# Three down products per gated chunk by a second level of Strassen's seven products

## The chip, the cores and the metric

The kernel runs on one core of a Trainium2 chip. The metric is device time in microseconds (us) for one execution, the median of several. The profile is of one execution of the same program; its durations are read against its own span.

## The reference

Four layers run over x, 2048 tokens of width 1024: attention, gated, attention, gated. Each adds to x what it computes from the LayerNorm of x.

```python
def _A_ref(x, wqkv, wo):            # linear attention, 32 heads of 32
    q, k, v = ...                   # (x @ wqkv), split into heads
    phi = lambda t: jnp.where(t > 0, t + 1, jnp.exp(t)) + 1e-6
    pq, pk = phi(q), phi(k)
    kv = jnp.einsum("bhsd,bhse->bhde", pk, v)
    z = jnp.einsum("bhsd->bhd", pk)
    num = jnp.einsum("bhqd,bhde->bhqe", pq, kv)
    den = jnp.einsum("bhqd,bhd->bhq", pq, z)[..., None] + 1e-6
    return (num / den) @ wo         # heads joined again

def _B_ref(x, W_gate, W_up, W_down):     # F = 3584
    gate = x @ W_gate
    gate = gate * (gate > 0)
    return (gate * (x @ W_up)) @ W_down

x = x + _A_ref(_layernorm(x), ...)
x = x + _B_ref(_layernorm(x), ...)
x = x + _A_ref(_layernorm(x), ...)
x = x + _B_ref(_layernorm(x), ...)
```

## The kernel before, in words

`run` (L1274) takes the layers in order: `layer_A(0)`, `layer_B(1)`, `layer_A(2)`, `layer_B(3)`. The residual x stays in SBUF as sixteen tiles of 128 tokens (L145), f32, 1024 wide.

A gated layer (`layer_B`, L1212) works on two chunks c = 0, 1 of 1024 tokens each. A chunk has two stages. In the gate/up stage a loop over u = 0 to 13 calls `glu` (L1063): each u makes 2 x 128 columns of F for both weights, with Strassen's seven products on blocks of 4 contraction tiles, and leaves four 128x512 blocks of h = relu(gate) * up in a tile hT[u // 2], f16, kept transposed (F on partitions, tokens on columns). So h has four blocks: a = first 512 tokens with the first half of F (in the order of the weight's tiles), b = first tokens, second half, g and d = the same for the second 512 tokens.

Then `down` (L1146) multiplies h by W_down, again with one level of Strassen: the chunk's 1024 x 3584 by 3584 x 1024 is cut into 2 x 2 blocks each way, and seven block products are summed. A product, `product` (L1168), is 4 banks (one per 128 tokens) x 14 contraction tiles = 56 matmuls of 128x128 by 512 columns, in two halves of 7 tiles, one ring entry per half. Their names: "11", "21", "22" use blocks of W_down as they are, T1, T2, T3, T4 use sums of weight blocks, made once in layer 1's chunk 0 (`sums_d`, L1002) and stored in DRAM as `td`. The order is 11, 21, T1, T2, T3, 22, T4. Product 11 goes to banks X, which ScalarE copies to banks Y (`seed`); 21 adds to X; T2, T3 and T4 add to Y; T1 and 22 use four banks V. After a product that completes a result, or a part of one, `add_down` (L1261) adds each bank onto x with one VectorE add of 512 columns, or in the last layer forms a bf16 tile and sends it out. VectorE makes the sums of h's blocks at the start of down (L1156 to L1159): e1 = g + d, e2 = e1 - a, and a - g in place of g, and after product 21 has read it b - e2 in place of b (L1193).

What sets the order: TensorE's instructions keep program order. The framework orders the other engines' queues by when things become ready, except where `issue_after` ties an instruction behind another one or a manual schedule is named. A list of later tasks (`_Later`, L71) runs host-side closures a number of ticks later; a tick is one small group of matmuls, 8 per down product. All weights come through one ring (`_Ring`, L24), depth 5: at the start of an entry's use, the load of the entry four ahead is issued on SP's queue, as soon as a slot is free. Ring entries, h, sums, transposed LayerNorm outputs and others share one pool of 16 slots of 8 KB per partition (`big`). SP's queue also takes the DMA transposes of LayerNorm's output (L397) and copies of x rows to DRAM and back (`send_away`, `bring_back`). PSUM has eight banks: four in `ps`, two in `ps3`, two in `kvp`.

In layer 1, chunk 1, the gate/up stage also makes weight sums for layer 2's projections (`load_w`, `sums_w`, L1015 and L1024): eight VectorE sums of 2048 elements, each placed behind the last put of h.

Of the kernel before, what the change touches and what calls it, by code (L numbers as in the profile page):

```python
# [8 lines left out]
ALU = mybir.AluOpType  # L9
ACT = mybir.ActivationFunctionType  # L10
F32 = mybir.dt.float32
BF16 = mybir.dt.bfloat16
F16 = mybir.dt.float16
PSUM = bass.MemoryType.PSUM
P = 128
NW = 512
HD = 32
QT = 4
# [5 lines left out]
class _Ring:  # L24


    def __init__(self, nc, slot, depth):
        self.nc, self.slot, self.depth = nc, slot, depth
        self.plan, self.tiles, self.loaded = [], {}, 0
# [63 lines left out]
class _Net:  # L93
    def __init__(self, tc, ctx, x_d, wqkv_d, wo_d, wg_d, wu_d, wd_d, out_d):
        nc = tc.nc
        self.tc, self.nc = tc, nc
        _, S, D = x_d.shape
        self.S, self.D = S, D
        self.ST, self.KT = S // P, D // P
        self.G = D // P  # L100
        self.F = wg_d.shape[1]
        self.FT = self.F // P
        self.NQ = self.ST // QT
        self.x_v = x_d.rearrange("b (st p) d -> p (b st) d", p=P)
        self.o_v = out_d.rearrange("b (st p) d -> p (b st) d", p=P)
        self.wqkv_v = wqkv_d.rearrange("(kt p) n -> p kt n", p=P)
        self.wo_v = wo_d.rearrange("(kt p) n -> p kt n", p=P)
        self.wgu_v = {"g": wg_d.rearrange("(kt p) f -> p kt f", p=P),
                      "u": wu_d.rearrange("(kt p) f -> p kt f", p=P)}
        self.wd_v = wd_d.rearrange("(u h p) n -> p h u n", p=P, h=2)  # L110
        self.U = self.F // (2 * P)

        pool = lambda name, bufs, **kw: ctx.enter_context(tc.tile_pool(name=name, bufs=bufs, **kw))
        self.const = pool("const", 1)
        self.xres = pool("xres", 1)
        self.big = pool("big", 16)
        self.ep = pool("ep", 7)
        self.small = pool("small", 4)
        self.ps = pool("ps", 4, space=PSUM)
        self.ps3 = pool("ps3", 2, space=PSUM)  # L120
        self.kvp = pool("kvp", 1, space=PSUM)


        self.spill = pool("spill", 1, space=bass.MemoryType.DRAM)
        self.NS = self.ST // 2
        self.ring = _Ring(nc, self.slot, 5)
        self.tgu = {(w, u): self.spill.tile([P, 4, NW], F16, name=f"t{w}{u}")
                    for w in "gu" for u in range(self.U)}
        self.td = self.spill.tile([P, self.U, 4, NW], F16, name="td")
        self.tw = {n: self.spill.tile([P, 8, NW], F16, name=f"t{n}") for n in ("q0", "q1", "k0", "k1")}  # L130
        self.later = _Later()
        self.phi_lag = 0

        from concourse.masks import make_identity
        self.ident = self.const.tile([P, P], BF16, name="ident")
        make_identity(nc, self.ident[:, :])
        self.ones = self.const.tile([P, P], BF16, name="ones")
        nc.vector.memset(self.ones, 1.0)
        self.mean = 2.0 ** -11
        assert self.S == 2 ** 11  # L140
        self.eps6 = self.const.tile([P, 1], F32, name="eps6")
        nc.vector.memset(self.eps6, 1e-6)
        self.eps5 = self.const.tile([P, 1], F32, name="eps5")
        nc.vector.memset(self.eps5, 1e-5)
        self.x = [self.xres.tile([P, D], F32, name=f"x{t}") for t in range(self.ST)]  # L145

        self.xb = [x[:, D // 2:D].bitcast(BF16) for x in self.x]
        self.xnT, self.xn, self.pk, self.slabs, self.xs, self.acc = {}, {}, {}, {}, {}, {}
        self.away = [self.spill.tile([P, D], F32, name=f"away{t}") for t in range(self.ST)]
# [803 lines left out]
    def plan_B(self, l):  # L953
        for c in range(2):
            for u in range(self.U):
                for w in "gu":
                    self.ring.add((l, c, w, u), lambda t, w=w, u=u, first=(l == 1 and c == 0):
                                  self.load_gu(t, w, u, first))
            for p in ("11", "21", "T1", "T2", "T3", "22", "T4"):
                for h in range(2):  # L960
                    us = slice(h * self.U // 2, (h + 1) * self.U // 2)
                    if p[0] == "T":
                        src = self.td[:, us, self.T_AT[p], :]
                    else:
                        n = int(p[1]) - 1
                        src = self.wd_v[:, int(p[0]) - 1, us, n * NW:(n + 1) * NW]
                    self.ring.add((l, c, p, h), lambda t, src=src: self.nc.sync.dma_start(
                        out=t[:, 0:self.U // 2, :].bitcast(src.dtype), in_=src))

    T_AT = {"T1": 0, "T3": 1, "T4": 2, "T2": 3}  # L970

    def raw_gu(self, t):
        return t[:, 0:4, :].rearrange("p a (b f) -> p (a b) f", f=2 * P)
# [89 lines left out]
    def glu(self, l, c, u, hT):  # L1063
# [74 lines left out]
        for w in "gu":  # L1138
# [4 lines left out]
            else:  # L1143
                put(2, Y[w])

    def down(self, l, c, hT, final):  # L1146


        nc, later, ring, v = self.nc, self.later, self.ring, self.nc.vector
        N = NW  # L1150
        pairs = [(p, [x[:, b::4, :] for b in range(4)]) for p, x in enumerate(hT)]
        e1, e2 = ([self.slot(f"e{i}_{l}_{c}_{k}", dtype=F16) for k in range(2)] for i in (1, 2))
        part = lambda e, p: e[p // 4][:, (p % 4) * 2:(p % 4) * 2 + 2, :]
# [6 lines left out]
        raw = lambda b: lambda k: hT[k // 2][:, (k % 2) * 4 + b, :]  # L1160
        own = lambda e: lambda k: e[k // 8][:, k % 8, :]
        X = [self.ps.tile([P, N], F32, tag="a", name=f"dx{j}") for j in range(QT)]
        Y = [self.ps3.tile([P, N], F32, tag="b", name=f"dy{j}") for j in range(2)]
# [48 lines left out]
    def layer_B(self, l, final):  # L1212
        ring = self.ring

        def behind(it, fn):
            with self.tc.issue_after(it.ins):
                fn()

        for c in range(2):
            hT = []  # L1220
            first = l == 1 and c == 0
            wd = {}
            for u in range(self.U):
                if u % 2 == 0:
                    hT.append(self.slot(f"h{l}_{c}_{u // 2}", dtype=F16))
                ring.load_to(ring.index((l, c, "g", u)) + 5)
                if first:
                    if u + 1 < self.U:
                        self.later.at(4 if u else 9, lambda u=u: behind(self.last_put if u else self.last_z, lambda: [
                            self.make_gu(ring.get((l, c, w, u + 1)), w, u + 1) for w in "gu"]))  # L1230
                    if u in (3, 7):
                        d = self.U - 4 + u // 4 * 2
                        wd[d] = self.load_d(d)
                    if 3 < u < 12:
                        self.later.at(4, lambda d=self.U - 4 + (u - 4) // 4 * 2, n=(u - 4) % 4: behind(
                            self.last_put, lambda: self.sums_d(wd[d], d, (n,))))
                if not final and c == 1:
                    if u in (0, 3):
                        self.load_w("qk"[u // 3])
                    if u in (1, 2, 4, 5):  # L1240
                        for n in range(2):
                            self.later.at(4 + 5 * n, lambda w="qk"[u // 4], n=2 * (u % 3 - 1) + n: behind(
                                self.last_put, lambda: self.sums_w(w, n)))
                if c == 0 and u == 1:
                    for n, turn in enumerate(self.turns):
                        self.later.at(1 + n, turn)
                if c == 0 and u in (1, 2):
                    self.later.at(6, lambda u=u: behind(self.last_put, self.pairs[u - 1]))
                self.glu(l, c, u, hT)
                if c == 0 and u == 2:  # L1250
                    self.pairs[2]()
                if c == 0 and u == (self.U - 1 if first else 0):
                    after = self.last_put.ins
            if c == 0:
                self.ln_chunk(l, 1, 20, 3, 3, after)
            elif not final:
                self.ln_later(l + 1, 0, 28, 3, 4)
                self.ln_later(l + 1, 1, 40, 3, 4)
            self.down(l, c, hT, final)
# [71 lines left out]
```

## Time and profile before

| | |
|---|---|
| median of 3 runs | 1461.36 us (1461.35 to 1461.69) |
| span of the profiled execution | 1459.6 us; the median lies 1.8 us above it |
| down, layer 1, chunk 1 | 650.84 to 735.44 us |
| down, layer 3, chunks 0 and 1 | 1117.79 to 1202.40 and 1371.61 to 1456.23 us |
| TensorE's clock granted | 1.00 |
| DMA | 268.09 MB, 184 GB/s on the mean |

Starts are from the span's start. In the group rows, "mean ns of one" is from an instruction's start to its end; neighbours on an engine overlap, so the pace of a stream is read from the chain or the timeline, as the difference of two starts. "Idle before" with an arrow names what released the engine.

### The profile page before, as it was taken

Reading aid. Unit: us, or ns where it says so; the run is one execution under the profiler, and the core shown is the slowest. Engines: PE = TensorE matmul, PEld = TensorE weight load, DVE = VectorE, ACT = ScalarE, POOL = GpSimd, SP = SyncE. Lnnn points to the kernel's source line nnn. Section 1 sums busy time; section 2 is a strip of 40 time slices with the busy share of each in tenths; the row PEclk is TensorE's granted clock in tenths of the full one; section 3 lists DMA queues with packets and bytes.
Section 4 is the critical chain, followed back from the end, with each engine's and each line's share of the span. In section 5 each row is a group of like instructions: output and inputs, shape, how many; then the busy total and the mean of one; then the engine's idle time right before and its main releaser. Section 6 shows DMA issues by size and latency. Waiting matters only on the chain.

```text
span 1459.6 us, 18713 instructions
## 1 busy us (share of the span) xinstructions
PE 1453.7 (100%) x6926; PEld 659.9 (45%) x6926; DVE 869.9 (60%) x1547; ACT 579.6 (40%) x1041; POOL 287.2 (20%) x190
## 2 busy tenths in 40 slices
PE   9999999999999999999999999999999999999999
PEld 4444444444444444444444444444444444444444
DVE  7978698666684554456388876776436433333632
ACT  7872564333340333340068626524333203333200
POOL 1454851011100011110031586401110001111000
PEclk9999999999999999999999999999999999999999
DMA  9840897564559996445943129975444787444461
GB/s 285 232 162 11 182 218 202 184 217 161 205 171 253 354 291 223 149 132 189 278 141 88 58 37 290 261 228 167 146 147 148 196 261 243 146 149 149 147 200 44
DMA packets 323915, 268.09 MB, mean 184 GB/s; under 512 B 106096, under 2 KB 295920, under 8 KB 321904
## 3 DMA queue, kind: packets, MB, share of 16 engines
q1 hardware_dynamic: 312800, 245.60, 57.2%
q10 hardware_dynamic: 11024, 21.30, 3.9%
q8 instruction: 54, 0.88, 0.3%
q14 instruction: 37, 0.30, 0.1%
HBM read 203.42 MB, written 38.80 MB: 166 GB/s over the span
## 4 chain that ended last, share of the span: by engine, by line
PE 96%; DVE 3%; ACT 1%; issue 0%; DMA 0%; DVEq 0%; ACTq 0%
PE ps L477 11%; PE dy L1177 10%; PE yu L1078 10%; PE yg L1078 10%; PE dv L1177 7%; PE dx L1177 7%; PE xg L1078 6%; PE xu L1078 6%; PE ps L755 4%; PE zg L1078 3%; PE zu L1078 3%; PE vu L1078 3%; PE vg L1078 3%; PE my L559 3%; PE mx L559 2%; PE mv L559 2%
## 5 line engine op out<-in xcount | busy, mean ns | idle before, releaser
L1078 PEld LDWEIGHTS <-w 128*128 128x128 f16 (+1 forms) x3136 | 306.6, 98 | 372.0 <-issue 2.5
L1131 POOL TENSOR_TENSOR h<-m5u,m5g 128x512 f16<-128x512 f32 x56 | 71.9, 1285 | 810.7 <-DVE m5u L1127 754.6
L477 PE MATMUL ps<-w,xnT 128*128 128x512 bf16 x768 | 169.8, 379 | 0.1
L1177 PEld LDWEIGHTS <-h 128*128 128x128 f16 x1120 | 109.6, 98 | 132.2
L1114 DVE TENSOR_TENSOR zg<-yg,m5g 128x512 f32<-128x512 f32 x56 | 39.1, 699 | 188.9 <-PE yg L1078 185.6
L1078 PE MATMUL yg<-s,w 128*128 128x512 f16 x448 | 115.0, 379 | 0.1
L1078 PE MATMUL yu<-s,w 128*128 128x512 f16 x448 | 115.0, 379 | 0.0
L1078 PE MATMUL xg<-xnT,w 128*128 128x512 f16 x448 | 115.0, 379 | 0.0
L1078 PE MATMUL xu<-xnT,w 128*128 128x512 f16 x448 | 115.0, 379 | 0.0
L477 PEld LDWEIGHTS <-xnT 128*128 128x128 bf16 x768 | 74.3, 98 | 89.8 <-issue 1.4
L1086 ACT ACTIVATE m5g<-m5g 128x512 f32<-128x512 f32 x56 | 35.2, 628 | 174.8 <-DVE m5g L1127 174.8
L1177 PE MATMUL dy<-w,h 128*128 128x512 f16 x448 | 98.0, 379 | 0.0
L1177 PE MATMUL dx<-w,h 128*128 128x512 bf16 x448 | 97.3, 379 | 0.0
L420 ACT ACTIVATE e<-e,eps 128x512 f32<-128x512 f32 x128 | 90.9, 720 | 3.3
L707 POOL TENSOR_TENSOR kvc<-pq,kvc 128x1024 f32<-128x1024 bf16 x32 | 78.6, 2455 | 53.1 <-DVE den L712 32.8
L755 PE MATMUL ps<-T,pqT 128*128 128x512 bf16 x384 | 83.6, 379 | 0.0
L1095 ACT ACTIVATE m5g<-vg 128x512 f32<-128x512 f32 x56 | 33.4, 597 | 110.9 <-PE vg L1078 85.2
L498 POOL TENSOR_TENSOR kvc<-kvc,slab 128x512 f32<-128x512 f32 x46 | 57.2, 1249 | 75.9 <-DVE slab L423 72.7
L1089 DVE TENSOR_TENSOR h<-yu,r 128x512 f16<-128x512 f32 x56 | 38.7, 691 | 56.0 <-PE yu L1078 56.0
L1127 DVE TENSOR_TENSOR m5u<-yu,m5u 128x512 f32<-128x512 f32 x56 | 38.7, 691 | 49.4 <-PE yu L1078 49.4
L1177 PEld LDWEIGHTS <-e 128*128 128x128 f16 x448 | 43.8, 98 | 52.9
L1086 ACT ACTIVATE r<-yg 128x512 f32<-128x512 f32 x56 | 33.4, 597 | 86.0 <-PE yg L1078 86.0
(198 smaller groups left out, 2129.9 us busy)
## 6 DMA issues: line engine op xcount, KB each, us to landing
w<-in_B_W_gate_dram SPq DMA_DIRECT2D x56, 512.0 KB, 5.9
w<-in_B_W_up_dram SPq DMA_DIRECT2D x56, 512.0 KB, 5.4
w<-td SPq DMA_DIRECT2D x32, 896.0 KB, 4.7
w<-in_B_W_down_dram SPq DMA_DIRECT2D x24, 896.0 KB, 5.2
w<-tg SPq DMA_DIRECT2D x42, 512.0 KB, 6.9
w<-tu SPq DMA_DIRECT2D x42, 512.0 KB, 6.7
w<-in_A_wqkv_dram SPq DMA_DIRECT2D x8, 1024.0 KB, 7.3
away<-x SPq DMA_DIRECT2D x16, 512.0 KB, 5.3
```

The lines of the kernel that those rows point to most:

```text
L420: nc.scalar.activation(out=e, in_=e, func=ACT.Exp, scale=-1.0, bias=self.eps6[:, 0:1])
L477: nc.tensor.matmul(by_row(ps), lhsT=self.xnT[l, l_q][:, kt, j * P:(j + 1) * P], rhs=w[:, kt, :].rearrange("p (b i d) -> p i b d", i=R, d=H ...
L498: nc.gpsimd.tensor_tensor(out=ksum[:, cols], in0=ksum[:, cols], in1=pk, op=ALU.add)
L559: nc.tensor.matmul(banks[j], lhsT=A(i)[:, j * P:(j + 1) * P], rhs=B(i), start=start and i == 0, stop=i == NS - 1, skip_group_check=True)
L707: nc.gpsimd.tensor_tensor(out=prod, in0=pq_of[sc, j], in1=zrow, op=ALU.mult)
L755: nc.tensor.matmul(ps, lhsT=pqT[sc][:, g, j * P:(j + 1) * P], rhs=T[g // 4][:, g % 4, n2 * NW:(n2 + 1) * NW], start=(g == 0), stop=(g == G ...
L1078: nc.tensor.matmul(ps, lhsT=W[w][m][:, k, :], rhs=A[m][:, k, :], start=start and k == 0, stop=k == 3, skip_group_check=True)
L1086: self.last_relu = nc.scalar.activation(out=out, in_=ps, func=ACT.Relu)
L1089: self.last_put = nc.vector.tensor_tensor(out=h[:, b, :], in0=ps, in1=R.pop(b), op=ALU.mult)
L1114: self.last_z = nc.vector.tensor_tensor(out=Z[w], in0=Y[w], in1=V[w], op=ALU.add)
L1131: nc.gpsimd.tensor_tensor(out=h[:, 3, :], in0=V["u"], in1=V["g"], op=ALU.mult)
L1177: nc.tensor.matmul(banks[j], lhsT=A(k)[:, j * P:(j + 1) * P], rhs=w[:, i, :], start=start and k == 0, stop=k == self.U - 1, skip_group_che ...
```

## The change

In three of the four gated chunks (all but layer 1's chunk 0) `down` calls a new `down_deep`. There T1, 22 and T4 are each computed by a second level of seven products. The block of h (512 tokens x 14 tiles) and the block of the weight (14 tiles x 512 columns) are cut in 2 x 2 again: an inner product is 2 banks' halves x 7 tiles = 14 matmuls of 128x128 by 256 columns, both 128-token halves in one bank. VectorE makes four inner sums of the h block, each in four pieces, into the space of h's block a, which is no longer needed after product 11. The order of the outer products becomes 11, 21, T1, T2, 22, T3, T4.

The inner weight sums (four per product) are made in layer 1's chunk 1, during gate/up: at u = 1, 4, 7 a weight block is loaded into two slots (`load_dd`), at u = 2, 3, 5, 6, 8, 9 two sums each are made (`sums_dd`) and stored in new DRAM tensors `dd`. A deep product takes four ring entries in place of two, seven DMAs in place of two. x becomes one SBUF tile with sixteen views, so that a put can add 2 x 256 columns of two token tiles at once.

```diff
+        self.dd = {p: self.spill.tile([P, 4, self.U // 2, NW // 2], F16, name=f"dd{p}") for p in self.DEEP}
...
-        self.x = [self.xres.tile([P, D], F32, name=f"x{t}") for t in range(self.ST)]
+        self.xall = self.xres.tile([P, self.ST, D], F32, name="x")
+        self.x = [self.xall[:, t, :] for t in range(self.ST)]
...
-            for p in ("11", "21", "T1", "T2", "T3", "22", "T4"):
+            for p in self.order_d(l, c):
+                if self.is_deep(l, c, p):
+                    for e in range(4):
+                        self.ring.add((l, c, p, e), lambda t, p=p, e=e: self.load_deep(t, p, e))
+                    continue
...
+    DEEP = ("T1", "22", "T4")
...
+    def sums_dd(self, p, n):
+        t = self.deep_t
...
+        self.nc.vector.tensor_tensor(out=out, in0=a, in1=b, op=ALU.subtract)
+        if n == 1:
+            self.later.at(2, lambda: [self.nc.sync.dma_start(out=self.dd[p][:, m, :, :], in_=f16(b))
+                                      for m, b in ((0, b11), (2, b12))])
...
+    def down_deep(self, l, c, hT, final):
...
+        def inner(A):
+            (a11, a21), (a12, a22) = ([cut(A[k], j) for j in range(2)] for k in range(2))
+            return (a11, a12, a21, a22), list(sums(((S1, a21, a22, ALU.add), (S2, S1, a11, ALU.subtract),
+                                                    (S3, a11, a21, ALU.subtract),
+                                                    (S4, a12, S2, ALU.subtract))))
...
+            def mm(m, A, bank, start=False):
+                for j in range(2):
+                    for i in range(NK):
+                        nc.tensor.matmul(bank[:, j * H:(j + 1) * H],
+                                         lhsT=A[i // 2][:, i % 2, j * P:(j + 1) * P], rhs=B[m](i),
+                                         start=start and i == 0 and j == 0, stop=i == NK - 1,
+                                         skip_group_check=True)
+
+            x, y, z = (self.ps.tile([P, N], F32, tag="a", name=f"d{n}{p}") for n in "xyz")
+            m5 = self.temp(name="dm5")
+            copy = lambda out, src: nc.scalar.activation(out=out, in_=src, func=ACT.Copy)
+            entry(0)
+            mm(1, a11, x, True)
+            copy(y, x)
+            later.tick()
+            mm(5, S1, z, True)
+            copy(m5, z)
+            later.tick()
+            entry(1)
+            mm(6, S2, y)
+            v.tensor_tensor(out=z, in0=y, in1=m5, op=ALU.add)
+            later.tick()
+            mm(2, a12, x)
+            put(0, 0, x, True)
+            put(1, 1, m5, False)
+            later.tick()
+            entry(2)
+            mm(7, S3, y)
+            put(1, 1, y, True)
+            later.tick()
+            mm(3, S4, z)
+            put(0, 1, z, True)
+            later.tick()
+            entry(3)
+            mm(4, a22, y)
+            put(1, 0, y, True)
+            later.tick()
...
+        product("11", raw(0), X, True, seed)
+        product("21", raw(1), X, False, to(first, 0, X, True))
+        for p, (_, b, _, _) in pairs:
+            v.tensor_tensor(out=b, in0=b, in1=part(e2, p), op=ALU.subtract)
+        parts, jobs = inner(of_e(e1))
+        for job in jobs:
+            job()
+        deep("T1", parts, put_both)
+        parts, jobs = inner(of_h(1))
+        spread(jobs, 1, 2)
+        product("T2", own(e2), Y, False, to(first, 1, Y, False))
+        deep("22", parts, put_into(first, 1))
+        parts, jobs = inner(of_h(3))
+        spread(jobs, 1, 2)
...
+        product("T3", raw(2), Y, False, third_done)
+        deep("T4", parts, put_into(second, 0))
...
+                if not final and c == 1:
+                    if u in (1, 4, 7):
+                        self.later.at(1, lambda p=self.DEEP[u // 3]: self.load_dd(p))
+                    if u in (2, 3, 5, 6, 8, 9):
+                        for n in range(2):
+                            self.later.at(2 + 5 * n, lambda p=self.DEEP[(u - 2) // 3], n=2 * ((u - 2) % 3) + n: behind(
+                                self.last_put, lambda: self.sums_dd(p, n)))
```

In `deep`, T1 puts each result onto both halves of the chunk (`put_both`, two adds), 22 and T4 onto one; `third_done` adds T3's banks onto two places. All of these are adds of 512 elements per partition onto x by VectorE, or the output tile in the last layer.

## The prediction

> **What bounds the kernel now.** I read the page's busy shares first, then the chain that ended last, then the groups with shapes kept apart, then the timeline and the stretches around the gated chunks' down products.
>
> ```profile
> PE 1453.7 (100%) x6926; PEld 659.9 (45%) x6926; DVE 869.9 (60%) x1547; ACT 579.6 (40%) x1041; POOL 287.2 (20%) x190
> PE 96%; DVE 3%; ACT 1%; issue 0%; DMA 0%; DVEq 0%; ACTq 0%
> 675.01 12.09 PE dv L1177 x56
> 147.92 0.89 PE kv L514 x16
> L514 PE MATMUL kv<-mt,w 128*128 128x128 bf16 x128 | 8.5, 219 | 0.0
> L514 PEld LDWEIGHTS <-w 128*128 128x128 bf16 x128 | 7.8, 98 | 1.9
> ```
>
> TensorE is the bound: busy all of the 1459.6 us, 96% of the chain. So matmul time taken away is span taken away, unless TensorE then waits. The durations (379 ns, 219 ns) are latencies that overlap; the pace is in the chain. One of the seven down products, 56 matmuls of 512 columns, takes 12.09 us, 215.8 ns each. The sixteen 128-column matmuls of L514 take 0.89 us, 55.6 ns each, each with its own weight load.
>
> ```profile
> 735.76 0.68 DVE L1265 TENSOR_TENSOR x<-x,dy 128x512 f32<-128x512 f32 x1
> 736.36 0.42 DVE L1053 TENSOR_TENSOR s<-s,xnT 128x512 f16<-128x512 f16 x1
> 736.70 0.69 DVE L160 BATCH_NORM_STATS2 stats<-x 128x6 f32<-128x512 f32 x1
> ...
> 499.84 1.22 DVE L1031 TENSOR_TENSOR wq<-wq,wq 128x2048 f16<-128x2048 bf16 x1
> 500.97 0.69 DVE L1114 TENSOR_TENSOR zu<-yu,m5u 128x512 f32<-128x512 f32 x1
> ...
> 501.72 1.02 PE L1078 MATMUL yu<-s,w 128*128 128x512 f16 x4
> ```
>
> This gives VectorE's pace: an f32 add of 512 holds the queue 0.60 us (done after 0.69), an f16 sum of 512 holds it 0.34. And it shows what a late bank costs: the 1.22 us sum pushed the zu add to 500.97, done 501.66, and TensorE went on at 501.72, 0.06 us later; its step before (zg at 500.69) should have ended at 501.55, so 0.16 us were lost.
>
> ```profile
> 675.00:687.00 12.00, 12.00 (x58) 5.45 (x56) 5.49 (x9) 0.00 (x0) 0.00 (x0) 1.00 0.47 154
> 518.00:530.00 12.00, 12.00 (x58) 5.46 (x56) 4.68 (x8) 4.67 (x8) 1.27 (x1) 1.00 1.09 349
> 578.00:590.00 12.00, 12.00 (x57) 5.42 (x56) 4.86 (x7) 4.58 (x9) 1.24 (x1) 1.00 0.55 175
> ```
>
> Columns: stretch, length, busy PE, PEld, DVE, ACT, POOL, clock, DMA share, GB/s. During product T1 of layer 1 VectorE works 5.5 of 12 us. In the gate/up part of the same chunk DMA is full (1.09 at 349 GB/s) early and half full (0.55, 175 GB/s) later.
>
> **Removed: matmul time.** Nine products (T1, 22 and T4 in three chunks) go from 56 matmuls of 512 columns to 7 x 2 x 7 = 98 of 256. No row of the trace has 256 columns. Between L514's 55.6 ns and L1177's 215.8 ns the straight line gives 109.0 ns, 98 x 109.0 = 10.68 us, 1.40 us saved per product, **12.6 us in all**. The rule that speaks against this: the Trainium skill, "TensorE: Matmul & The Clock Gate", section "Back-to-back issue gap", says that a stream of weight load and matmul pairs sustains only about 81 ns at 128 columns, not 56. By that rule 256 columns would cost about 109 + 25 = 134 ns (an estimate from that page), a product 13.1 us, and the change would lose 9 us before anything else. The row has such pairs at 55.6 ns, so I take 109; but it has only 16 in a row, so the rule stays as a rival.
>
> **Added on VectorE in down.** Per chunk 24 adds onto x become 33 plus 3 into z and 3 more for T3's second target, 39 (15 more, 9.0 us), and 48 inner sums come (per product twelve of 0.34 and four of 256 elements, about 0.20 by the same slope: 4.8 us, 14.4 in three). VectorE had 46 us in the 84 us of down in layer 1; with 23 more it still fits, but not everywhere. The built program's VectorE order places T1's inner sums before product 21's adds (they need only product 11 to be over): 21 sums of 1024 at 0.60 and these 4.8 us end about 18 us into the 24 us of 11 and 21. Hidden; without that cover TensorE would wait up to 5 us there, three times.
>
> What is not hidden are the banks used again inside a deep product, with steps of 1.53 us in the order 1, 5, 6, 2, 7, 3, 4. Step 7 writes the bank that the z add after step 6 reads; step 4 writes the one that the put after step 7 reads. The spare step between is 1.53 us, and ahead of both reads other work stands in VectorE's queue. Walk T1 of layer 3, t from its first matmul, 0.2 us from a step's end to VectorE's start (1137.47 against 1137.27 in the timeline): leftovers of 21 (four h updates at 0.60 and one add) last to 2.3; the S1 sums for product 22, which wait for step 5 (3.25), to 4.45; two puts of m5 to 5.65; z done at 6.34. Step 7 is due at 6.10, goes at 6.40: 0.3 lost. Then three S2 sums to 7.25, two puts of x to 8.45, two sums to 9.0, two puts of y, done 10.27; step 4, due 9.46, goes at 10.33: 0.87 lost. Together 1.17. T1 of layer 1 has two statistics in place of sums: 0.89. Product 22 puts once, not twice: z done 6.41 (0.37 lost), y done 9.56 (0.09): 0.46. T4 has no sums beside it: 0. Sum: 0.89 + 2 x 1.17 + 3 x 0.46 = **4.6 us back**. Queued behind those waits are only puts and sums that T2 and T3, 12 us each on other banks, absorb.
>
> Product 22 moves ahead of T3: its h blocks were updated during T1, and T3's banks then have a whole product in which T2's adds read them; down has 53 ticks instead of 56, so LayerNorm's steps and their transposes on SP shift by a tick or two, with layer 2's first use of them after the end of down. Cost 0.
>
> ScalarE gets two copies of 0.58 us per product. Each has the 1.53 us of the next step as cover, and LayerNorm's 1.24 us activations stand behind them in its order; cost 0. POOL does nothing in down.
>
> **Added in layer 1, chunk 1, gate/up.** Twelve sums of 1792 elements for the stored inner weights; from L1031's 1216 ns for 2048, about 1.08 us, 0.99 in the queue. In the place where L1031 lost 0.16 us a 0.99 us sum loses 0.03, so by themselves 0.4 at most. But each waits for its load, and VectorE's puts wait behind it. The loads and stores are 3 x (1.8 + 1.8) MB, some 11 MB, on SP's queue among the ring's loads, in a stretch whose first half is already at 350 GB/s. Following SP's order at 350 GB/s, every "up" block still lands 2 to 7 us before its turn; the second raw pair (22) lands near 545.4 and 547.9, while the sums stand ahead of a z add due at 547.1. I take 1.0 us. Ends: 0 (all in time; I see no gain) and 8 us (each of three pairs some 2.7 us late).
>
> **Added DMA in down.** A deep product brings 3.1 MB, not 1.8, in seven DMAs in place of two: 4 MB more in 80 us per chunk. A ring load is issued four entries ahead; deep entries last 3 us, so the lead falls from 24 us to 10.7 at least. Rows of 512 bytes are no novelty: the 512 KB gate blocks land in 5.9 us. What gets close is the hand-over to the next stage: layer 2's k0 is now issued when T4 starts, 10.7 us ahead (35 us before the change), with a landing of 8.7 us in that stretch, and transposes of about 2 us each stand between k0 and k1 on SP. I take 0.6 us for both hand-overs; ends 0 and 5. At the very end the last add is split in two as before: 0. Making x one tile leaves the waits of the other stages as they were in the built order: 0.
>
> Sum against the profiled execution: 1459.6 - 12.6 + 4.6 + 1.0 + 0.6 = 1453.2 us of span. The median lies 1.8 us above that span, so **1455.0 us**. About 0.2% (2.9 us) is what a measurement of this kernel can tell from no change.
>
> **Rivals.** (A) As summed, 1453 to 1458: 0.50. (B) The banks come free in time, since the order in the queue bends with real landings: stalls under 1.5 us and no late DMA, 1448.8 to 1452: 0.18. For it: T4's pattern loses nothing; against: the walk has 5 to 6 us of queue between steps 5 and 7. (C) DMA: the stored sums and the hand-over take most of the bounds above, 5 to 10 us, as the share of 1.0 and more suggests: 1458.4 to 1464: 0.18. Against: the ring's 12 to 24 us of lead. (D) The slower one, a single mechanism: the 256-column stream is paced by its weight loads. A product breaks even at 12.09/98 = 123 ns, the whole change at (9 x 12.09 - 6.2)/882 = 116 ns. At the skill's 134 ns: 9 x (13.13 - 12.09) = +9.4, with 6.2 of stalls 1477: 0.14 with all that goes with it (several late DMAs beyond their bounds, 1465 and more). That fewer columns are not streamed is excluded: the built program has 756 more TensorE rows, that is 9 x 42 pairs.
>
> Chances: faster by over 0.2% (below 1458.4) 0.68, within 0.2% 0.18, slower 0.14. The range takes in A, B and C: 1449 to 1464.5.
>
> **What would show it.** In the changed profile: 256-column matmuls of T1, 22 and T4, with T4 at 10.7 us in the chain (right) or 12 and more (D); TensorE waiting on VectorE's z add and puts in T1 and 22, about 0.5 to 1.2 us each, and none in T4 (A), or none anywhere (B); in layer 1's gate/up, steps of 12.25 us at two to four units and not more, else VectorE waiting for the loads of the inner sums (C); no TensorE wait on layer 2's k0. I am wrong if a deep product costs over 12 us, or if the stalls come to less than 2 or more than 9 us.

## The result and the profile after

The changed kernel takes **1455.34 us** (median of 5 runs, 1455.16 to 1456.68) against 1461.47 (5 runs, 1461.35 to 1462.16): ratio 0.996, 95% interval 0.9947 to 0.9972. Its profiled execution has a span of 1453.6 us and took 1455.34 us itself. Predicted were 1453.2 and 1455.0. The total is as forecast; several of its terms are not, and the experiments below are about those. In what follows a *put* is an add of a finished bank onto x (or into the output tile xo), m5 is ScalarE's copy of step 5's bank, and the *z add* is VectorE's sum of step 6's bank y and m5.

The page of the changed kernel, its busy shares and the shares of the chain that ended last:

```profile
PE 1442.2 (99%) x7304; PEld 696.9 (48%) x7304; DVE 952.4 (66%) x1748; ACT 589.9 (41%) x1059; POOL 288.9 (20%) x190
...
PE 88%; DVE 7%; issue 1%; SPq 1%; DMA 1%; ACT 1%; DVEq 0%; ACTq 0%
```

TensorE has 11.5 us less to do, and the chain now leaves it for 12% of the span instead of 4%: other engines have come onto the path. The chain in layer 1's T4 shows the pace (start, length, what):

```profile
724.06 1.53 PE dyT L1308 x14
725.59 1.53 PE dxT L1308 x14
727.12 1.53 PE dyT L1308 x14
```

From start to start a step is 1.5285 us, so 14 matmuls of 256 columns take 109.2 ns each and 98 of them 10.70 us, where the prediction had 109.0 and 10.68. What TensorE waits for, after (engine and line, what released it: us in total, times, longest; before there was only the wait at the start and three of 0.2 to 0.3):

```profile
PE dyT L1308 <- ACT dyT L1315: 1.5, 1, 1.5
PE idle L278 <- DVE e L275: 1.3, 1, 1.3
PE qy L663 <- DVE qz L685: 1.0, 1, 1.0
PE dyT L1308 <- DVE x L1269: 0.9, 3, 0.5
PE dy L1308 <- DVE dz L1325: 0.8, 1, 0.8
```

Three kinds are new: one wait for ScalarE's copy (L1315) in a T4, VectorE's adds in T1 (L1269) and in product 22 (L1325), and one outside down, layer 2's qy waiting for qz (L685). The wait view counts idle time behind the last matmul's modelled end. From here on a **loss** is the distance between two neighbouring matmuls' starts beyond the pace: for these rows 1.68, 1.19, three T1 losses of 0.32 to 0.65, and 0.95 (two more of T1, 0.33 and 0.07, are at step 7). The largest T1 loss, at step 4 in layer 3's first chunk, ends when the second of two puts of y is done (1149.57); VectorE, then TensorE:

```profile
1148.30 1.27 DVE L1269 TENSOR_TENSOR x<-x,dyT 128x512 f32<-128x512 f32 x2
...
1149.62 1.69 PE L1308 MATMUL dyT<-w,e 128*128 128x256 f16 x14 [0.49 <-DVE x L1269]
```

The ledger, all from the first matmuls' starts in the two traces (us; the last stage ends one pace after the last matmul's start):

| stage | before | after | difference |
|---|---|---|---|
| up to down of layer 1, chunk 1 | 650.67 | 650.46 | -0.21 |
| that down | 84.61 | 81.08 | -3.53 |
| layer 2 and gate/up of layer 3, chunk 0 | 382.35 | 383.82 | **+1.47** |
| down of layer 3, chunk 0 | 84.61 | 83.77 | **-0.84** |
| gate/up of layer 3, chunk 1 | 169.21 | 169.21 | 0.00 |
| down of layer 3, chunk 1 | 84.61 | 80.88 | -3.73 |
| behind the last matmul | 3.54 | 4.34 | **+0.80** |

A down with three deep products and no loss would be 84.61 - 3 x 1.40 = 80.4. Two of the three come within 0.7 of that; the middle one gives 3.4 us back, and layer 2 gives 1.5 back that nobody touched. Those two were the question.

**Down of layer 3, chunk 0.** ScalarE's timeline at the beginning of T4 (ACTq is its queue issuing transfers), the same four transfers by themselves (shortest, median and longest issue in ns, first and last start), and VectorE's timeline in T3:

```profile
1183.14 7.66 ACTq L1277 DMA_DIRECT2D out_dram<-xo  x4
1190.85 0.58 ACT L1315 ACTIVATE dyT<-dxT 128x512 f32<-128x512 f32 x1 [13.46 <-DMA out_dram<-xo]
...
L1277 ACTq DMA_DIRECT2D out_dram<-xo x4: 338/348/352, 1183.1 to 1190.5; - x4
...
1186.35 0.42 DVE L1118 TENSOR_TENSOR s<-xnT 128x512 f16<-128x512 f16 x1 [2.64 <-DMA xnT<-xnb]
...
1189.75 0.68 DVE L1276 TENSOR_TENSOR xo<-x,dy 128x512 bf16<-128x512 f32 x1
```

The copy that step 6 needs was due at 1188.4, when step 1 ended. It stands in ScalarE's queue behind four output transfers of T3. The 7.66 us of the first row are not the cost of issuing: one issue takes 0.35 us, and the rest is waiting. Each transfer waits for the put that makes its tile xo; the fourth put ends at 1190.43, its transfer is issued at 1190.46, the copy begins at 1190.85. Three of the four puts were late because VectorE had waited 2.64 us, until 1186.35, for a transpose of normalised rows, which a sum for the *next* chunk's gate/up needs. So the chain runs from a late transpose through VectorE's and ScalarE's queues to TensorE. Without that wait the fourth put could have ended near 1187.6 (T3's last matmul starts at 1186.54; 0.22 us for it, 0.2 to VectorE's start, 0.68 for the put), and the copy would have been in time; that is an estimate, and no run takes away this wait alone. And VectorE's timeline around product 22:

```profile
1162.32 0.42 DVE L1118 TENSOR_TENSOR s<-xnT 128x512 f16<-128x512 f16 x1
1163.91 0.42 DVE L1118 TENSOR_TENSOR s<-xnT 128x512 f16<-128x512 f16 x1 [1.17 <-DMA xnT<-xnb]
...
1169.34 0.69 DVE L1325 TENSOR_TENSOR dz<-dy,dm 128x512 f32<-128x512 f32 x1
```

VectorE waits 1.17 us for another of these transposes, with product 22's inner sums and its z add (L1325, done 1170.03) queued behind; step 7 starts at 1170.08.

**The beginning of layer 2.** The timeline of VectorE, ScalarE and TensorE there:

```profile
731.54 0.41 DVE L1118 TENSOR_TENSOR s<-xnT 128x512 f16<-128x512 bf16 x1
...
745.54 0.30 ACT L169 ACTIVATE rstd<-mv,eps 128x1 f32<-128x1 f32 x1 [2.09 <-DVE mv L167]
...
752.80 0.69 DVE L425 SCALAR_TENSOR_TENSOR x<-ps,e 128x512 bf16<-128x512 f32 x1 [1.60 <-ACT e L422]
753.41 0.69 DVE L685 TENSOR_TENSOR qz<-qy,qm 128x512 f32<-128x512 f32 x1
...
754.15 1.02 PE L663 MATMUL qy<-w,s 128*128 128x512 f16 x4 [1.03 <-DVE qz L685]
```

Read backwards: qy waits for qz, which stands behind an L425, which waits for ScalarE's e, and ScalarE had waited 2.09 us for statistics (mv) from VectorE, with the e steps behind that wait in its queue. VectorE was late with mv because layer 2's sixteen sums (L1118 to L1121, 0.34 us each) began at 731.54, at the very end of down; before the change they began at 728.79, 6.5 us before its end, with all four puts of T4's results still to come:

```profile
728.79 0.43 DVE L1052 TENSOR_TENSOR s<-xnT 128x512 f16<-128x512 bf16 x1 [3.65 <-PE dy L1177]
```

That was a reading, not yet a proof.

### The profile page after: what moved, and what is told of

Read it like the earlier page. It is cut to its first block, busy times and chain, and to the rows that moved or that the text cites. A ratio compares the mean times of both kernels' runs of the same rounds, so it can differ in the third digit from the quotient of the medians.

```text
span 1453.6 us, 19842 instructions
## 1 busy us (share of the span) xinstructions
PE 1442.2 (99%) x7304; PEld 696.9 (48%) x7304; DVE 952.4 (66%) x1748; ACT 589.9 (41%) x1059; POOL 288.9 (20%) x190
## 4 chain that ended last, share of the span: by engine, by line
PE 88%; DVE 7%; issue 1%; SPq 1%; DMA 1%; ACT 1%; DVEq 0%; ACTq 0%
PE yg L1144 10%; PE yu L1144 10%; PE ps L479 10%; PE xu L1144 6%; PE xg L1144 6%; PE ps L757 4%; PE zu L1144 3%; PE dx L1256 3%; PE zg L1144 3%; PE dy L1256 3%; PE vu L1144 3%; PE vg L1144 3%; PE my L561 3%; PE dy L1418 2%; PE mv L561 2%; PE mx L561 2%
## 5 line engine op out<-in xcount | busy, mean ns | idle before, releaser
L1308 PEld LDWEIGHTS <-h 128*128 128x128 f16 x756 | 74.0, 98 | 13.1 <-issue 3.0
L1256 PEld LDWEIGHTS <-h 128*128 128x128 f16 x504 | 49.3, 98 | 58.6
L1256 PE MATMUL dx<-w,h 128*128 128x512 bf16 x336 | 73.0, 379 | 0.0
L421 ACT ACTIVATE e<-ps 128x512 f32<-128x512 f32 x92 | 54.2, 589 | 29.1 <-PE ps L479 28.9
```

The lines of the kernel that those rows point to most:

```text
L421: nc.scalar.activation(out=e, in_=ps, func=ACT.Relu, scale=-1.0)
L1256: nc.tensor.matmul(banks[j], lhsT=A(k)[:, j * P:(j + 1) * P], rhs=w[:, i, :], start=start and k == 0, stop=k == self.U - 1, skip_group_che ...
L1308: nc.tensor.matmul(bank[:, j * H:(j + 1) * H], lhsT=A[i // 2][:, i % 2, j * P:(j + 1) * P], rhs=B[m](i), start=start and i == 0 and j == 0 ...
```

## The experiments

Each is an edit of the changed kernel unless it says otherwise. "Own span" is that of the profiled execution, to be set against 1453.6; a median is that of its timed runs.

**Output transfers on POOL's queue**

```diff
-            for k, queue in zip(range(m) if split else (0,), (nc.scalar, nc.sync)):
+            away = nc.scalar if ts.start >= second and cols.start == 0 else nc.gpsimd
+            for k, queue in zip(range(m) if split else (0,), (away, nc.sync)):
```

> Edit to the changed kernel: the output transfers of the deep down products, except those of T4 at the end, are issued from POOL's queue instead of ScalarE's. Theory (ScalarE's copy of dyT waits behind output transfers that ScalarE issues and that wait for lanes): T4 of layer 3's first chunk loses nothing at its step 6, the wait of TensorE on L1315 (1.5 us once, 1.68 us between matmul starts) is gone, and the span is 1.5 to 1.7 us shorter, about 1452. Rival (the copy is late because ScalarE's LayerNorm work or its own input is late): the wait stays at 1 us or more and the span at 1453.6. Second rival (POOL's issues write their descriptors more slowly, and take the lanes from the transposes at another time): T4's wait goes but a wait of similar size comes at the hand-over or in product 22.

Own span 1451.6, median 1453.33 (ratio to before 0.9944, 0.9932 to 0.9957). ScalarE's timeline at T4:

```profile
1188.66 0.58 ACT L1316 ACTIVATE dyT<-dxT 128x512 f32<-128x512 f32 x1 [15.62 <-PE dxT L1309]
```

The copy is now released by TensorE's own step and done at 1189.24, 0.75 us before step 6 starts (1189.99); T4's loss is gone. Product 22's loss grew from 0.95 to 1.57 (down 82.44 after 83.77), as the second rival had half foreseen: VectorE's wait for the transpose is 1.78 us here. That the copy is late by standing behind the transfers is shown; that these "wait for lanes", as the expectation has it, is not what the rows say: they wait for VectorE's puts. Layer 2 (383.82) did not move.

**m5's adds on POOL**

```diff
             copy(m5, z)
+            put(1, 1, m5, False, nc.gpsimd)
...
-            put(1, 1, m5, False)
```

> Edit: the add of m5 onto x (twice in T1, once in 22 and T4) is made by POOL right after ScalarE's copy of m5, not by VectorE after step 2. Theory (the stalls before steps 7 and 4 come from what stands ahead in VectorE's queue): T1's stalls of 0.64, 0.71 and 0.44 us lose at least half, about 1 us of the span, none appears elsewhere, span about 1452.6; POOL's adds take about 1.2 us each. Rival (POOL's add and VectorE's get in each other's way, or the put of y then waits for POOL): T1's stalls stay or grow by up to 1 us each and VectorE's adds in T1 take over 0.75 us; span 1454 or more.

Own span 1457.5, median 1459.05: 3.9 us of span worse, the rival. Every T1 lost more (1.87 at step 4 in layer 1, 1.50 at step 7 twice in layer 3). The timeline of POOL and VectorE in layer 3's first T1:

```profile
1145.30 2.68 POOL L1269 TENSOR_TENSOR x<-x,dm 128x512 f32<-128x512 f32 x2 [28.45 <-ACT dm L1315]
...
1145.55 2.71 DVE L1283 TENSOR_TENSOR h<-h 128x512 f16<-128x512 f16 x2 [0.23 <-PE dyT L1308]
```

Two f16 sums that take 0.42 us elsewhere took 1.30 and 1.49: each lasted until POOL's add beside it had ended (1.27 and 1.45 us long). The Trainium skill, "SBUF — State Buffer", section "SBUF: two separate sides", has it so: a GpSimd operation that reads SBUF and a VectorE operation with two SBUF inputs take a shared port pair in turn, for a whole instruction. The rows agree with it (POOL's add starts first both times, and VectorE's sum ends 0.28 us after it), and an "idle" POOL is no free adder beside VectorE's sums. So this run says nothing of whether T1's losses come from VectorE's queue; two later ones do.

**LayerNorm three ticks earlier**

```diff
-                self.ln_later(l + 1, 0, 28, 3, 4)
-                self.ln_later(l + 1, 1, 40, 3, 4)
+                self.ln_later(l + 1, 0, 25, 3, 4)
+                self.ln_later(l + 1, 1, 37, 3, 4)
```

> Edit: LayerNorm for the next layer's first eight row tiles is begun 3 ticks earlier in the down products that end a layer (28 to 25, 40 to 37), as much as down lost in ticks (56 to 53). Theory (the 1.46 us lost after layer 1's down comes from LayerNorm steps that now fall later against the q and k products and fill VectorE's and ScalarE's queues there): layer 2's waits on qx and qy shrink by 1 us or more, span about 1452.3. Rival (the loss comes from the order in which the work of layer 2's beginning itself is queued, or from the shifted loads): the waits at qx and qy stay within 0.3 us, span 1453.4 to 1454; or the statistics then wait for adds onto x that are not done, and a stall of 0.5 us or more appears in layer 1's 22 or T4.

Own span 1454.3, median 1456.07. Layer 2 to 0.01 us as it was (383.81; losses of 0.28 and 1.19 at the same two matmuls). The theory of the shifted ticks fell: down's 53 ticks instead of 56 are not what costs the 1.47 us.

**T1 as one product**

```diff
-    DEEP = ("T1", "22", "T4")
+    DEEP = ("22", "T4")
...
-        deep("T1", parts, put_both)
+        product("T1", own(e1), V, True, t1_done)
```

> Edit: T1 by one product of 56 matmuls again, with the stored inner sums of T1 and their sums left out; 22 and T4 stay deep. Theory (T1's stream gives 1.40 us per chunk and its stalls take 1.79 of 4.20 in three): three T1 products at 12.09 us without stalls, span about 2.4 us longer, 1456.0; gate/up of layer 1's second chunk unchanged within 0.2 us. Rival one (T1's load of VectorE also causes the later stalls in 22 and T4 and at the hand-over, and its DMAs the late transposes): these shrink too and T1 is worth less than 1 us, span under 1454.6. Rival two (the stored sums of T1 cost in gate/up): that part gets shorter by 0.5 us or more.

Own span 1454.8, median 1457.10. The three downs: 81.83, 83.89, 81.83 instead of 81.08, 83.77, 80.88, in all 1.8 us longer, not 2.4. In the first and third the sum holds: 1.40 less T1's losses there (0.64 and 0.44). In the middle one T1 is worth only 0.12: 22's loss of 0.95 is gone (the transposes then come in time for VectorE), T4's copy is later by 0.38 (2.06). So rival one is right for that chunk: the deep T1 is what makes the transposes late for VectorE, whether by its shorter time, its loads or its work on VectorE this run doesn't separate. Gate/up was 0.2 us later than in the changed kernel, so the stored sums of T1 cost nothing there that shows.

**T4 in matmuls of 128 columns**

```diff
+                        for n in range(2 if p == "T4" else 1):
+                            s = slice(n * P, n * P + P) if p == "T4" else slice(0, H)
...
-                        nc.tensor.matmul(bank[:, j * H:(j + 1) * H],
+                            nc.tensor.matmul(bank[:, j * H + s.start:j * H + s.stop],
```

> Edit: in T4 of the three chunks every 256-column matmul is issued as two of 128 columns, each with its own load of the same 128 x 128 block: 196 pairs in a row where there were 98, same columns streamed. Theory (pace set by columns, 55.6 ns at 128 as in L514's sixteen): T4 takes 196 x 55.6 ns = 10.9 us, 0.2 us more, span about 1454.2. Rival (a stream of weight load and matmul pairs holds only about 81 ns at 128 columns, the Trainium skill, TensorE: Matmul & The Clock Gate, section Back-to-back issue gap): T4 takes about 15.9 us, span about 1469.

Own span 1455.0, median 1456.78. TensorE's timeline in layer 3's last T4, 28 pairs to a step:

```profile
1440.31 1.73 PE L1310 MATMUL dxT<-w,h 128*128 128x128 f16 x28
1441.88 1.73 PE L1310 MATMUL dzT<-w,h 128*128 128x128 f16 x28
1443.44 1.73 PE L1310 MATMUL dyT<-w,h 128*128 128x128 f16 x28
```

1.564 us between starts is 55.8 ns a pair; down of layer 1 and of layer 3's second chunk took 0.25 us more each, where 0.2 was expected from the columns and 5.2 by the rule. The page's 81 ns doesn't hold for this stream of 196 pairs. (The rest of the 1.4 us is elsewhere: a wait of 1.4 for layer 2's output weights and 22's loss at 1.82.)

**Layer 2's sums in T3**

```diff
-                self.ln_later(l + 1, 0, 28, 3, 4)
-                self.ln_later(l + 1, 1, 40, 3, 4)
+                self.ln_later(l + 1, 0, 24, 2, 4)
+                self.ln_later(l + 1, 1, 32, 2, 4)
+                for j in range(QT):
+                    self.later.at(40 + 2 * j, lambda j=j: self.sums_x(l + 1, 0, j))
```

> Edit: the sixteen sums of layer 2's normalised rows (16 x 0.34 us on VectorE) are issued at ticks 40 to 46 of layer 1's last down product instead of ticks 1 to 4 of layer 2, and LayerNorm of the first eight row tiles starts at ticks 24 and 32, two ticks apart, so that their rows are there. Theory (T4's puts, now spread over T4, stand ahead of these sums in VectorE's queue; they begin at 731.5 and so LayerNorm's statistics for the last rows come late, ScalarE waits for them in order, and TensorE waits 1.19 us for the qz add): VectorE reaches the qz add in time, TensorE's waits on qx and qy at the beginning of layer 2 fall from 1.47 us to 0.3 at most, span about 1452.3. Rival one (the waits come from ScalarE's own load there): they stay within 0.3 us. Rival two (the sums then stand ahead of T3's or T4's puts): a stall of 0.5 us or more in product 22 or T4 of layer 1 gives it back.

Own span 1458.1, median 1459.23. Theory and rival two both came true: layer 2 takes 382.36 us, to 0.01 the 382.35 of before, with neither loss left; and T4 of layer 1 loses 4.75. (The edit moves LayerNorm as well as the sums.) The cost comes by a third engine, ScalarE's timeline:

```profile
726.09 0.29 ACT L169 ACTIVATE rstd<-mv,eps 128x1 f32<-128x1 f32 x1 [2.52 <-DVE mv L167]
...
727.36 0.29 ACT L169 ACTIVATE rstd<-mv,eps 128x1 f32<-128x1 f32 x1 [0.74 <-DVE mv L167]
...
727.79 0.58 ACT L1313 ACTIVATE dyT<-dxT 128x512 f32<-128x512 f32 x1
```

VectorE waited 4.06 us, until 716.91, for a transpose of these sums, the statistics (mv) stood behind it, ScalarE's rstd steps waited for mv, and T4's copy stood behind those. T4's copy again, with another thing ahead of it.

The wait had a second price. Down takes 87.37 us, 6.29 more, of which the wait is 4.75. In the 3.2 us behind it TensorE's granted clock (the 0.50 below, third figure from the end) is half of what it is elsewhere, and 14 matmuls in a row take about 0.21 us each instead of 0.11:

```profile
728.40:731.60 3.20, 3.18 (x16) 2.19 (x16) 1.35 (x3) 0.48 (x1) 0.00 (x0) 0.50 0.98 311
```

After the first microseconds of the program such a stretch stands in three of the fourteen traces only, each time within 0.9 us behind a loss of over 3 us (4.75 here, 3.18 and 3.47 in two runs below), and it lasts 3 to 3.5 us. Behind losses of up to 2.06 us the pace stays.

**Layer 3's sums in T3**

```diff
+            more = (9, 4, 1, 0)[j] if l == 3 else 0
-            self.later.at(first + (2 * j + 1) * step + lag + 3, lambda j=j: self.sums_x(l, c, j))
+            self.later.at(first + (2 * j + 1) * step + lag + 3 + more, lambda j=j: self.sums_x(l, c, j))
```

> Edit: in layer 3's first chunk the sums over the next chunk's normalised rows are issued 9, 4, 1 and 0 ticks later, that is in T3 and not at T2's end. Theory (VectorE waits 1.17 us at 1163.9 for a late transpose, with product 22's inner sums and its z add behind it in the queue): product 22's stall of 0.95 us goes, VectorE's wait on the transpose too, span about 1452.7; T4's wait for ScalarE's copy stays at 1.5. Rival (product 22's own queue of puts and inner sums is what is late, as the prediction summed): a stall of 0.4 us or more stays at step 7, and the sums moved between the puts add one at step 4.

Own span 1456.3, median 1456.93. 22's loss is gone altogether, so the theory of 22 holds. It agrees with the sizes in the other runs: where VectorE waited 1.17, 1.78, 2.04 and 2.17 us for the transpose (the changed kernel, transfers on POOL, T4 in 128 columns, T1 put once), 22 lost 0.95, 1.57, 1.82 and 1.94. But T4's copy was not "at 1.5":

```profile
PE dyT L1309 <- ACT dyT L1316: 3.0, 1, 3.0
```

The sums moved into T3 took their waits with them: VectorE waited 5.15 and 1.36 us for transposes there, T3's last put into xo ended at 1192.00, and the copy began at 1192.42 instead of 1190.85. The loss grew from 1.68 to 3.18, and the lower clock behind it (0.56 from 1193.0 to 1196.5) cost 1.6 more: this down takes 86.00. A further 1.0 us of the span lies ahead of layer 1's down, which the edit doesn't touch.

**The three together**

```diff
+            away = nc.scalar if ts.start >= second and cols.start == 0 else nc.gpsimd
...
+                    self.later.at(40 + 2 * j, lambda j=j: self.sums_x(l + 1, 0, j))
...
+            more = (9, 4, 1, 0)[j] if l == 3 else 0
```

> Edit: the output transfers on POOL's queue, the early sums of layer 2 and the later sums of layer 3 together. If the three losses are independent: 1.7 (T4's copy, already seen to go), 1.2 (layer 2's beginning) and 0.95 (product 22; 1.57 with the transfers moved), in all about 4 us below the changed kernel, span 1449.3 to 1450, time about 1451.3. Rival (they share one cause, the lanes' load, and moving one moves another): less than 2.5 us in all, 1451.1 or more of span.

Own span 1454.0, median 1457.99, the rival's number but not its cause: the middle down takes 81.28 (-2.5) and layer 2 382.35 (-1.5), both repaired, and layer 1's T4 loses 3.47 to the early sums and 1.7 more to the lower clock behind that wait (down 86.21).

**Without the early sums**

The first and third edit of the run before alone.

```diff
+            away = nc.scalar if ts.start >= second and cols.start == 0 else nc.gpsimd
...
+            more = (9, 4, 1, 0)[j] if l == 3 else 0
```

> Edit: of the three in the run before, only the output transfers on POOL's queue and the later sums of layer 3; layer 2's sums stay where the changed kernel has them. Theory (product 22's stall comes from the sums that wait on a late transpose, T4's from ScalarE's copy behind output transfers; early sums of layer 2 only moved a wait into T4 of layer 1): layer 3's first down product about 81.3 us instead of 83.8, layer 2's waits on qx and qy 1.47 us as in the changed kernel, T4 of layer 1 without a stall, span about 1450.7, time 1452.3. Rival (the transfers and the transposes share lanes, and the gain moves): 1451.6 or more, as with the transfers alone.

Own span 1450.6, expected 1450.7; the middle down 81.22, layer 2 383.95. The median of the timed runs is 1453.68 (1452.40 to 1455.19), so the profiled one was the fastest of them.

**T1 put once**

```diff
         def put_both(j, h, src, last):
-            for a in range(2):
+            for a in range(1):
```

> Edit to the changed kernel: T1 is put onto its first target only, the puts onto the second are left out (a part of the computation is missing: five adds of 0.60 us on VectorE in each T1, the second use of T1). Theory (T1's stalls of 0.64, 0.71 and 0.44 us are VectorE's queue of double puts and inner sums): they fall to 0.1 at most, span about 1451.9. Rival (the stalls come from what TensorE's own order places next to them, T2's and T1's loads landing late, or ScalarE's copies): they stay within 0.2 us of what they are.

Own span 1452.0, expected 1451.9; median 1453.88. T1's losses: 0.26 at step 7 in layer 1, 0.13 there in layer 3's first chunk, 0.39 where they were 1.79 (at most 0.1 each was expected). So the queue of puts is most of what T1 loses by, as the prediction's walk had it, though with other sizes. That the span agrees is in part chance: 22 lost 0.99 more (the transposes again, for which VectorE now waited longer), T4's copy 1.13 less. The latter speaks for the chain read above: VectorE's wait for the transpose in T3 ended at 1185.21 here, 1.14 us earlier.

**Layer 2's sums behind T3's last add**

On the run without the early sums; `t3_add` is the last add onto x that `onto` issued.

```diff
-                self.ln_later(l + 1, 0, 28, 3, 4)
-                self.ln_later(l + 1, 1, 40, 3, 4)
+                self.ln_later(l + 1, 0, 24, 2, 4)
+                self.ln_later(l + 1, 1, 32, 2, 4)
+                for j in range(QT):
+                    self.later.at(46 + j, lambda j=j: self.behind(self.t3_add, lambda j: self.sums_x(l + 1, 0, j), (j,)))
```

> Edit: as the run with two edits, and layer 2's sums issued at ticks 46 to 49 of layer 1's last down product, behind T3's last add in VectorE's queue, so that the statistics for layer 2's first half rows and their ScalarE steps stand ahead of them; LayerNorm of the first eight row tiles at ticks 24 and 32, two apart. Theory (the early sums cost a stall in T4 because statistics, and with them ScalarE's rstd steps ahead of its copy, stood behind sums that waited for transposes): T4 of layer 1 loses 0.5 us at most, layer 2's waits on qx and qy stay under 0.3, span about 1449.5 to 1450, 1 us under the run with two edits. Rival (VectorE's work at the hand-over is simply too much for the time, wherever it stands): what goes from qx and qy comes back in T4 or later in layer 2, span within 0.4 us of the run with two edits.

Own span 1449.5, median 1451.99 (1451.26 to 1453.92; ratio to before 0.9938, 0.9925 to 0.9950). Layer 2 takes 382.36, and layer 1's T4 loses 0.39. What TensorE still waits for on VectorE in down:

```profile
PE dyT L1308 <- DVE dzT L1325: 0.7, 3, 0.3
PE dyT L1308 <- DVE x L1268: 0.7, 3, 0.3
```

So the hand-over's 1.47 us was the place of sixteen sums in VectorE's queue, not too much work: put where the statistics and ScalarE's steps stand ahead of them, they cost next to nothing. LayerNorm moved with them here; three ticks of LayerNorm alone had changed nothing.

**T1's m5 puts last**

On the run before.

```diff
             put(0, 0, x, True)
-            put(1, 1, m5, False)
+            if p != "T1":
+                put(1, 1, m5, False)
...
             put(1, 0, y, True)
+            if p == "T1":
+                put(1, 1, m5, False)
```

> Edit: the run with layer 2's sums behind T3's last add, and in T1 the two puts of m5, which free no bank, follow the put after step 4 instead of standing ahead of the z add; nothing is left out. Theory (T1's stalls are the queue ahead of the adds that free a bank, 2 x 0.60 us of it m5): T1's stalls of 0.33, 0.32, 0.44 and 0.44 us fall to 0.1 at most each, span about 1448.2, time about 1450.5. Rival (what stands ahead is mostly the inner sums, or the two adds moved behind delay T2's adds and so the next product): 0.3 us or more stays in each T1, or a new wait in product 22; span 1449 or more.

Own span 1448.4, expected 1448.2; the three downs 81.14, 80.82 and 80.57. TensorE's longest waits but for the one at the start (two of 0.2 outside down follow):

```profile
PE qx L663 <- DVE qy L654: 0.3, 1, 0.3
PE ps L479 <- ACT xnT L337: 0.3, 1, 0.3
PE dyT L1308 <- DVE dzT L1325: 0.2, 1, 0.2
```

T1's losses at step 7 are gone; at step 4 0.31 is left in layer 1, and 0.13 in each chunk of layer 3 (from 0.44), where the theory had 0.1 at most. The median, 1452.05 (1450.26 to 1454.17; ratio 0.9938, 0.9925 to 0.9952), is that of the run before: the 1.1 us show in the profiled executions and drown in runs that scatter by 4 us, where those of before scatter by 1. Both versions have medians 3.3 us below the changed kernel's 1455.34 and 9.4 below before; the intervals of their ratios overlap that of the changed kernel (0.9947 to 0.9972) at its end only.

## Why the prediction was right in sum, and where not

Against the summed span of 1453.2, term by term: matmuls as said; banks used again -1.86; ScalarE's copies +1.68; gate/up -1.2; hand-over +0.9; behind the last matmul +0.8. Together +0.3. The matmul term is no luck; that the other errors, of 0.8 to 1.9 us each, cancel to 0.3 is.

- **Matmul time, -12.6: right.** 109.2 ns where 109.0 was drawn from L514's sixteen pairs and L1177's pace, and rival D is out by 882 matmuls at that pace, and by 196 pairs in a row of 128 columns at 55.8 ns.
- **Banks used again, +4.6: right mechanism, mis-sized.** 2.74 in all: T1 0.64, 0.71 and 0.44 for 0.89, 1.17 and 1.17; product 22 0, 0.95 and 0 for 0.46 each. The walk for layer 3 had 22's first inner sums begin when step 5 ends, at 3.25, and the z add done at 6.34; in the trace they begin at 2.71, while step 5 still runs, and the z add is done at 6.13 and 5.85. And one matmul of T2 stands ahead of T1's step 4, which covers 0.22 us: TensorE's queue too is not in program order everywhere, as it was taken to be. Putting T1 once and moving m5's puts both show the queue as T1's cause. (The adds in a down come to the 39 foreseen, but as 32, 3 and 4.) For 22 the step was wrong in kind: it loses nothing by its own puts, and 0.95 once by a late transpose ahead of it. "T4: 0" held for VectorE.
- **"Each has the 1.53 us of the next step as cover ...; cost 0": failed.** The copy's cover is 1.53 us, and I looked only at activations that might stand ahead of it. Two other things do in ScalarE's queue, both waiting for VectorE: output transfers that wait for their puts and, in the runs with early sums, rstd steps that wait for statistics. It cost 1.68 us, shown by moving the transfers. That the puts were late by a transpose is read from the trace, and agrees with the runs that put T1 once and moved layer 3's sums. "T4 has no sums beside it: 0" missed the next chunk's sums, which reach T4 in this way.
- **Layer 1's gate/up, +1.0: too dear.** -0.21; the loads of the inner weights came in time for VectorE's queue. The slips of 0.16 us stay at two units and are gone at two others, and one of 0.10 is new. The stretches show the extra work taken up (VectorE 4.68 and 4.86 of 12 us before; columns as in the prediction's):

```profile
518.00:530.00 12.00, 12.00 (x57) 5.47 (x56) 6.86 (x10) 4.67 (x8) 1.28 (x1) 1.00 1.08 360
578.00:590.00 12.00, 12.00 (x57) 5.41 (x56) 7.04 (x9) 4.67 (x8) 1.27 (x1) 1.00 0.98 299
```

- **Hand-overs, +0.6: about the place, wrong in cause.** I gave k0's and k1's loads; neither is waited for. "LayerNorm's steps ... shift by a tick or two ... Cost 0" was nearer to it and also not it, since three ticks changed nothing. The cost is a queue order that came with the change: T4's puts, formerly four in its last 6 us, are spread over it, and layer 2's sums now stand behind all but the last of them, not ahead. It is 1.47 us, shown by moving the sums with LayerNorm ahead of them (382.36); why the framework orders the queue so was not tried.
- **"At the very end ...: 0": left open.** +0.80. The last add's end is as before, and it is the last transfer that ends later. Over the runs here whose end is untouched this part took 3.54 to 4.80 us, so a single profile can't give it to the change.
- Rival B's picture (no stalls, about 1449) is what the last two edits make of the kernel. Rival C's price didn't come through the ring, but DMA is in it twice, as late transposes ahead of product 22's z add and of T3's puts.

## What to carry to other kernels

When the bound engine is made faster, the covers of everything timed against it shrink: list for each step that must finish within one such cover what stands *ahead* of it in its own queue, transfers issued there and waits of small operations included, and what *these* wait for, not only how long it takes itself. Put output transfers on the queue of an engine that nobody waits for at that time, and adds that free a buffer ahead of adds that don't. When work is spread differently over a stage, look at what used to slip in between at its end. And keep single waits of the bound engine short: here each of over 3 us brought 1.5 to 1.7 us of slow matmuls with it.

## What the runs showed of the hardware

An output transfer of 128 KB in ScalarE's queue took 0.35 us to issue, and began 0.03 us after the VectorE add that made its data; while four of them waited for their adds, from 1183.14 to 1190.85, ScalarE computed nothing, and the copy behind them stood. With the transfers on POOL's queue the copy began 0.2 us after TensorE's step. An f16 sum of 512 elements on VectorE took 1.30 and 1.49 us instead of 0.42 beside POOL's f32 adds. Weight load and matmul pairs of 128 columns held 55.8 ns over 196 in a row. Behind losses of 3.18, 3.47 and 4.75 us TensorE's matmuls ran at half their pace for 3 to 3.5 us, with a granted clock of 0.50 over the 3.2 us behind the longest; behind losses of up to 2.06 us they did not.
